# Loading two token tiles as one 2 KB-packet transfer on the second DMA queue, and two weight row blocks as one

## The chip, the cores and the metric

The kernel runs on one NeuronCore of one Trainium2 chip. The metric is the device time of one execution in microseconds, as the median of several runs. Besides, one execution was taken by the hardware profiler; its instructions and transfers are what the profile shows.

## The reference

With x of 2048 tokens by 512 (bf16), the output mixes two branches by a gate for each token:

```python
g = sigmoid((x * gate_w).sum(-1, keepdims=True))
a = A_ref(x, A_wqkv, A_w_phi, A_wo)     # linear attention, 32 heads of 16, softmax feature maps
b = relu(x @ B_w1) @ B_w2               # B_w1: 512 x 1376, B_w2: 1376 x 512
return g * a + (1 - g) * b
```

In A_ref, q, k and v come from x @ wqkv; q and k are multiplied by w_phi for each head and mapped to softmax(p) and softmax(-p), 32 features for each head; then kv is the sum over tokens of phi_k times v, z the sum of phi_k, and the head's output is (phi_q kv) / (phi_q z + 1e-6), which wo projects. Every token's row of the output depends on its own row of x and on sums over all tokens (kv and z), so the order in which tokens stand in a tile does not matter as long as the output rows are put back where they belong.

## The kernel before

The 2048 tokens are 16 tiles of 128, in four chunks of 512. The kernel wants x transposed (XT: features on the partitions). Chunks 1 to 3 come by transposing DMAs (x1, x2, x3). Chunk 0 is wanted first and goes another way: its four tiles m = 0 to 3 are loaded as they are (x00 to x03, into XN, which lies in a buffer FT that is used for other things later), TensorE multiplies each 128 x 128 block by the identity (xt{m}0 and xt{m}1, line 350), ScalarE and VectorE copy the result from PSUM to XT (xe{m}0, line 362, and xe{m}1, line 365).

The first matrix product is h = x W1. W1 is loaded in pieces: columns 0 to 511 by row blocks of 128 (w1a0 to w1a3, 128 KB each), then columns 512 to 1023 in one load of 512 KB (w1b), then the rest (w1c). For the first 256 tokens and the first four column blocks the sum over the row blocks j is spread out, so that TensorE can begin with what has landed: hh00 and hh01 (row block 0, tiles 0 and 1), then hh1, hh2 and hh3 (row blocks 1, 2 and 3 for both tiles; line 405). Then hr0, hr1 and h0_0 to h0_3 (line 411) do the other 256 tokens for these columns, tile 2 (and with it xe20 and xe21) being the first that hr0 needs. h0_4 and on (line 391) take whole chunks; f1_0 to f1_3 (line 374) are folds of the k projection with w_phi, and pr_k0 and on (line 512) the projections. Before any data are there, TensorE does six matmuls on constants (warm0, line 258).

Work is a list of named tasks. Each engine runs its tasks in an order written out by hand (ORDER, lines 17 to 62), and a task waits on semaphores for those tasks of other engines, and those DMAs, that it depends on. DMAs are issued by SP and by ScalarE ("act"), each with its own queue; the transposing loads, too, stand in SP's list. The orders that matter here begin so:

```python
    "sp":  "x00 w1a0 w1a2 x02 x03 w1b wphi wkT w1c wv x1 x2 wqT x3 gw w2a w2b wo ...
    "act": "x01 w1a1 w1a3 xe00 xe10 xe20 xe30 rl0_0 ...
    "pe":  "warm0 xt00 xt01 xt10 xt11 hh00 hh01 hh1 hh2 xt20 xt21 xt30 xt31 hh3 hr0 hr1 h0_0 ...
```

The list g.follow(...) at line 429 repeats part of the order as a constraint. Later parts (features on VectorE, ScalarE and GpSimd, kv, num and den, the output tiles oe{m} and their stores st{m} at line 692) are not touched, but for two stores' addresses. A buffer of stored outputs (OSB) has five slots.

Of the kernel before, what the change touches and what calls it, by code (L numbers as in the profile page):

```python
# [15 lines left out]

ORDER = {
# [4 lines left out]
    ),  # L22
# [5 lines left out]
    ),  # L28
    "act": (
# [20 lines left out]
    ),  # L50
# [98 lines left out]
def bass_gated_mix__linear_kernel_hedgehog__dense_activation_relu__prompt_kernel(  # L149
# [11 lines left out]
    x2 = A_x.rearrange("b s d -> (b s) d")  # L161
    o2 = out.rearrange("b s d -> (b s) d")
    S, D = x2.shape
    H, DH = A_w_phi.shape[0], A_w_phi.shape[1]
    DFF = B_w1.shape[1]
    P = 128
    NT = S // P
    ND = D // P
# [11 lines left out]
    NPB, NTS, NF, NSL = 3, 3, 4, 3  # L180
    NPH, NOM, NOT, NOS = 7, 3, 4, 5
# [6 lines left out]
    with ExitStack() as es:  # L188
        E = es.enter_context

        def sb(name, shape, dt):
            return E(nc.sbuf_tensor(name, shape, dt))
# [6 lines left out]
        W1 = sb("W1", [P, ND, W1C], BF16)  # L199
# [7 lines left out]
        FT = sb("FT", [P, NF, 2 * F], BF16)  # L207
# [3 lines left out]
        OSB = sb("OSB", [P, NOS, D], BF16)  # L211
# [20 lines left out]
        PS = E(nc.psum_tensor("PS", [P, 8, 512], FP32))  # L232
        EPS = 8 * 512

        def ap(t, row, off, dims):
            return bass.AP(tensor=t, offset=off, ap=[[row, P]] + [list(d) for d in dims])

        def psap(off, dims):
            return ap(PS, EPS, off, dims)

        g = _Graph()
        add = g.add
# [5 lines left out]
            boost=700.0)  # L248
        add("ones", "pool", lambda q: q.memset(
            ap(VS, NT * NG * GZ, GV, [[GZ, NT * NG], [1, 1]]), 1.0), dur=0.7, boost=-1e4)  # L250
        add("hpad", "pool", lambda q: q.memset(HR[:, :, :, KREM:P], 0.0), dur=0.6, boost=-1e4)
        XN = FT[:, NF - 2, :].rearrange("p (m d) -> p m d", d=D)
# [13 lines left out]
        def after_last(name, eng):  # L266
            if eng in queue:
                g.follow(queue[eng], name)
            queue[eng] = name

        def load(name, eng, out_, in_, deps=(), dur=0.1, lat=6.0, **how):
            add(name, eng, lambda q: q.dma_start(out=out_, in_=in_, **how), deps, dur=dur, lat=lat, dma=True,
                boost=1e4)
            after_last(name, eng)
# [6 lines left out]
        def chunk(c):  # L281
            return slice(c * 512, (c + 1) * 512)

        w1r = B_w1.rearrange("(j p) n -> p j n", p=P)
        x0r = x2[chunk(0), :].rearrange("(m p) d -> p m d", p=P)
        wvr = A_wqkv[:, 2 * D:3 * D].rearrange("(j p) n -> p j n", p=P)
        def load_x(m, eng, lat):
            load(f"x0{m}", eng, XN[:, m, :], x0r[:, m, :], dur=0.45, lat=lat)

        def load_w(j, eng, lat):  # L290
            load(f"w1a{j}", eng, W1[:, j, 0:512], w1r[:, j, 0:512], dur=0.45, lat=lat)
# [2 lines left out]
        load_x(1, "act", 3.1)  # L294
        load_w(0, "sp", 3.2)
        load_w(1, "act", 3.4)
        load_w(2, "sp", 3.8)
        load_w(3, "act", 3.95)
        load_x(2, "sp", 4.0)
        load_x(3, "sp", 3.9)  # L300
        load("w1b", "sp", W1[:, :, 512:1024], w1r[:, :, 512:1024], dur=0.5, lat=5.0)
        load("wphi", "sp", WPS[:, :, :], A_w_phi.rearrange("(g hl) r c -> (hl r) g c", g=ND), dur=0.5, lat=4.9)
        load_t("wkT", WT[:, ND:2 * ND, :], A_wqkv[:, D:2 * D], (), 4.1, 2.7)
# [21 lines left out]
            ("shift",), dur=0.2)  # L325
        add("mk", "dve", lambda q: q.tensor_tensor(
            MK[:, :], ROWM[:, :], ap(COLH, P, 0, [[DH, GH]]), ALU.is_equal), ("row4", "iota_c"), dur=0.2)
        for j in range(ND):
            add(f"wbd{j}", "dve", lambda q, j=j: q.tensor_tensor(
# [18 lines left out]
        def pe_xt(q, m, n):  # L348
            for j in range(2 * n, 2 * n + 2):
                last = q.matmul(PS[:, XB[m][j // 2], (j % 2) * P:(j % 2 + 1) * P], XN[:, m, j * P:(j + 1) * P],  # L350
                                IDN[:, :], start=True, stop=True)
            return last

        for m in range(4):
            for n in range(2):
                add(f"xt{m}{n}", "pe", lambda q, m=m, n=n: pe_xt(q, m, n),
                    (f"x0{m}", "ident", f"xe{m - 2}{n}" if m > 1 else None), dur=0.2, boost=9000.0 - 10 * m)
            for n, eng in enumerate(("act", "dve")):
                xo = XT[:, 2 * n:2 * n + 2, m * P:(m + 1) * P]
                xi = PS[:, XB[m][n], 0:2 * P].rearrange("p (j t) -> p j t", j=2)  # L360
                if eng == "act":
                    add(f"xe{m}{n}", eng, lambda q, o=xo, i=xi: q.activation(o, i, ACT.Copy), (f"xt{m}{n}",), dur=0.35,
                        boost=9000.0 - 10 * m)
                else:
                    add(f"xe{m}{n}", eng, lambda q, o=xo, i=xi: q.tensor_copy(o, i), (f"xt{m}{n}",), dur=0.37,
                        boost=9000.0 - 10 * m)
        x0 = [f"xe{m}{n}" for m in range(4) for n in range(2)]
# [35 lines left out]
        def pe_h_first(q, j, c0, c1):  # L403
            for k in range(4):
                last = q.matmul(PS[:, GB4[k], c0:c1], W1[:, j, k * P:(k + 1) * P], XT[:, j, c0:c1],  # L405
                                start=(j == 0 and c0 == 0), stop=(j == ND - 1), skip_group_check=True)
            return last
# [10 lines left out]
        add("hh01", "pe", lambda q: pe_h_first(q, 0, P, 2 * P), ("xe10", "hh00"), dur=0.22, boost=8500.0)  # L418
        prev = "hh01"
        for j in range(1, ND):  # L420
            add(f"hh{j}", "pe", lambda q, j=j: pe_h_first(q, j, 0, 2 * P), (f"xe0{j // 2}", f"xe1{j // 2}", f"w1a{j}", prev), dur=0.44,
                boost=8500.0)
            prev = f"hh{j}"

        for k in range(2):
            add(f"hr{k}", "pe", lambda q, k=k: pe_h_rest(q, k, 2 * P, 3 * P, True), ("xe20", "xe21", prev), dur=0.22,
                boost=8200.0)
            prev = f"hr{k}"
        for line in (("warm0", "xt00", "xt01", "xt10", "xt11", "hh00", "hh01", "hh1", "hh2", "xt20", "xt21", "xt30", "xt31",
                      "hh3", "hr0", "hr1"), ("xe00", "xe10", "xe20", "xe30"),  # L430
                     ("ident", "shift", "xe01", "xe11", "xe21", "xe31", "blk", "row4", "mk")):
            for a, b in zip(line, line[1:]):
                g.follow(a, b)
# [8 lines left out]
        for n, (kind, a, k) in enumerate(units):  # L442
            b = GB4[n] if n < 4 else FB[2] if n == 4 else HB[(n - 4) % len(HB)]
            if kind == "h":
                halved = n < 4
                deps = [*xof[a], *w1of[k], prev, *freed[b]]
                if k == KT - 1:
                    deps.append("gw")
                    add(f"h{a}_{k}", "pe", lambda q, a=a, b=b: pe_h_tail(q, a, b), deps, dur=0.69)
                    prev = f"h{a}_{k}"  # L450
# [4 lines left out]
                        out=HT[:, KT - 1, chunk(a)].rearrange("p (n t) -> p n t", t=P),  # L455
                        in_=HR[:, a % 2, :, :].rearrange("p n k -> p (n k)")),
# [9 lines left out]
                    deps, dur=(0.22 if k < 2 else 0.44) if halved else 0.87,  # L466
                    boost=8000.0 if n < 3 else 0.0)
                prev = f"h{a}_{k}"
# [3 lines left out]
            else:  # L472
                deps = ["wqT", *wbd, prev, *freed[b]]
                add(f"f{a}_{k}", "pe", lambda q, a=a, k=k, b=b: pe_fold(q, a, k, b), deps, dur=0.24, boost=1000.0)
                prev = f"f{a}_{k}"
# [4 lines left out]
        for j in range(ND):  # L480
# [3 lines left out]
                boost=1800.0)  # L484
# [11 lines left out]
        for m in range(NT):  # L496
            def add(*a, boost=20.0 * (len(widths) * 2 - m // 2 - VLAG), **how):
                return g.add(*a, boost=boost, **how)
# [18 lines left out]
        for jn, (kind, tiles) in enumerate(jobs):  # L517
            w = len(tiles)
            n = kind_n[kind]
# [59 lines left out]
            else:  # L579
# [4 lines left out]
                    dur=0.11 + 0.207 * w)  # L584
# [6 lines left out]
                for n2, m in enumerate(tiles):  # L591
                    add(f"tq{m}", "sp", lambda q, m=m, fs=fs, n2=n2: q.dma_start_transpose(
                        out=PHQ[:, m % NPH, :, :], in_=FT[:, fs, n2 * F:(n2 + 1) * F]),
                        (f"nm_{J}", *((f"nd{m - NPH}_0", f"nd{m - NPH}_1") if m >= NPH else ())), dur=1.3, lat=2.3, dma=True)
                    if n2 == 0 and m == 0:

                        for b in range(2):
# [9 lines left out]
                                out=o, in0=i, scalar=5e-7, in1=k, op0=ALU.add, op1=ALU.mult),  # L607
                                (f"kv{NT - 1}", "mk"), dur=0.2)
                for m in tiles:
                    for hf in range(2):  # L610
# [3 lines left out]
                        def pe_nd(q, m=m, hf=hf, nb=nb):  # L614
# [11 lines left out]
                            out=OTM[:, m % NOM, hf * 256:(hf + 1) * 256].rearrange("p (h d) -> p h d", d=DH),  # L626
# [4 lines left out]
                        out=OT[:, m % NOT, :, :], in_=OTM[:, m % NOM, :]),  # L631
# [17 lines left out]
                    if m == NT - 1:  # L649
# [15 lines left out]
                        for h2 in range(2):  # L665
# [13 lines left out]
                            else:  # L679
                                add(f"oe{m}_1", "dve", lambda q, m=m, b=b, cs=cs: q.tensor_scalar(  # L680
                                    OSB[:, m % NOS, cs], PS[:, b, 0:cs.stop - cs.start], OMG[:, m:m + 1], None, ALU.mult), need,
                                    dur=0.4)
                            add(f"st{m}_{h2}", ("act", "sp")[h2], lambda q, m=m, cs=cs: q.dma_start(
                                out=o2[m * P:(m + 1) * P, cs], in_=OSB[:, m % NOS, cs]), (f"oe{m}_{h2}",), dur=0.5,
                                lat=1.5, dma=True)
# [4 lines left out]
                        OSB[:, m % NOS, :], PS[:, ab, :], ACT.Copy, scale=OMG[:, m:m + 1]),  # L690
                        (f"a{m}", f"go{m // 4}", f"st{m - NOS}" if m >= NOS else None), dur=0.69)
                    add(f"st{m}", "act", lambda q, m=m: q.dma_start(
                        out=o2[m * P:(m + 1) * P, :], in_=OSB[:, m % NOS, :]), (f"oe{m}",), dur=0.5, lat=1.5, dma=True)

        for then in ("mx_k0", "mn_k0"):
            g.follow("mk", then)
# [41 lines left out]
```

## Time and profile before

| what | value |
|---|---|
| median of 3 runs | 150.18 us (150.1 to 150.44) |
| profiled execution, its own time | 150.59 us |
| its span from first to last instruction | 149.3 us |
| TensorE busy | 146.3 us, 98% of the span |
| VectorE, ScalarE, GpSimd busy | 110.9, 91.8, 109.6 us |
| granted TensorE clock | 1.00 |
| DMA | 16.11 MB, mean 108 GB/s |

In the lines of the profile a time comes first (start in us from the span's begin, then the length), then the engine, the line of the kernel, the operation, the tiles (out<-in, W standing for W1, W2 and the like) and the count; in brackets stands the idle time of the engine before it and what ended it. "SPq" and "ACTq" are the queues' issues of DMAs, PE is TensorE's matmul and PEld its weight load. The DMA view gives the kilobytes and the time from issue to landing. A line of windows has, for each engine, the busy time and the number of instructions, then the granted clock, the busy share of the 16 DMA engines and GB/s.

### The profile page before, as it was taken

To read this page: it belongs to the slowest core of one execution; us is meant where nothing else is said; L and a number is where in the kernel's file an instruction comes from. 1 tells how busy PE (TensorE), PEld (TensorE's weight loads), DVE (VectorE), ACT (ScalarE), POOL (GpSimd) and SP (SyncE) were. 2 spreads that over 40 slices of the span, in tenths; PEclk is the share of its full clock that TensorE was granted. 3 is DMA by queue.
4 is the path that set the end of the run, shared out by engine and by line. 5 is a ranking of instruction groups with operands and counts; after the bars stand their busy time and mean duration, and the time that the engine had idled before them with its cause. 6 is when DMAs were issued, how large, how long until landed. Compare 5 with 4: busy or idle time off the path is not lost.

```text
span 149.3 us, 2619 instructions
## 1 busy us (share of the span) xinstructions
PE 146.3 (98%) x1009; PEld 75.9 (51%) x1009; DVE 110.9 (74%) x168; ACT 91.8 (61%) x127; POOL 109.6 (73%) x72
## 2 busy tenths in 40 slices
PE   7999999999999999999999999999999999999994
PEld 2865444444754465445444545455444444445452
DVE  2343666999796948989999997999989988534401
ACT  3374769799979775898983937175573751310151
POOL 4000399999999999999999999999999793150000
PEclk9999999999999999999999999999999999999999
DMA  5999999900030001000000094646778687656552
GB/s 144 303 234 247 171 212 211 341 27 0 7 70 0 0 4 37 0 0 4 0 0 0 2 111 104 141 103 139 121 169 190 159 212 97 156 134 159 63 156 91
DMA packets 46364, 16.11 MB, mean 108 GB/s; under 512 B 39856, under 2 KB 46352, under 8 KB 46352
## 3 DMA queue, kind: packets, MB, share of 16 engines
q1 hardware_dynamic: 43616, 13.50, 43.2%
q10 hardware_dynamic: 2736, 2.45, 5.1%
q8 instruction: 8, 0.13, 0.4%
q14 instruction: 4, 0.03, 0.1%
HBM read 4.41 MB, written 2.10 MB: 44 GB/s over the span
## 4 chain that ended last, share of the span: by engine, by line
PE 98%; DVE 0%; issue 0%
PE PS L638 24%; PE PS L391 21%; PE PS L512 19%; PE PS L492 9%; PE PS L644 9%; PE PS L573 3%; PE PS L616 3%; PE PS L399 2%; PE PS L405 2%; PE PS L258 2%; PE PS L659 2%; PE PS L411 1%; PE PS L374 1%; PE PS L350 1%; PE PS L670 1%; DVE OSB L680 0%
## 5 line engine op out<-in xcount | busy, mean ns | idle before, releaser
L552 POOL TENSOR_TENSOR TS<-PB,MX 128x1024 bf16<-128x1024 bf16 (+1 forms) x18 | 30.9, 1723 | 15.0 <-DVE MX L543 15.0
L638 PE MATMUL PS<-W,HT 128*128 128x512 bf16 (+1 forms) x165 | 38.1, 379 | 0.0
L559 DVE TENSOR_REDUCE ZB<-FT 128x128 f32<-128x2048 bf16 (+1 forms) x18 | 36.6, 2031 | 1.8 <-ACT FT L557 1.8
L557 ACT ACTIVATE FT<-TS 128x2048 bf16<-128x2048 bf16 (+1 forms) x18 | 30.9, 1718 | 8.7 <-POOL TS L552 8.5
L391 PE MATMUL PS<-XT,W 128*128 128x512 bf16 x144 | 34.7, 379 | 0.0
L552 POOL TENSOR_TENSOR TS<-MN,PB 128x1024 bf16<-128x1024 bf16 (+1 forms) x18 | 30.9, 1725 | 0.8 <-DVE MN L545 0.8
L512 PE MATMUL PS<-WP,XT 128*128 128x512 bf16 x128 | 30.6, 379 | 0.0
L566 POOL TENSOR_TENSOR FT<-FT,SC 128x2048 bf16<-128x2048 bf16 (+1 forms) x9 | 29.5, 3287 | 0.0
L469 ACT ACTIVATE HT<-PS 128x512 bf16<-128x512 f32 x40 | 22.6, 597 | 5.6 <-PE PS L391 4.6
L638 PEld LDWEIGHTS PS<-W,HT 128*128 128x128 bf16 (+1 forms) x165 | 15.5, 98 | 17.1
L689 ACT ACTIVATE OSB<-PS,OMG 128x512 bf16<-128x512 f32 x15 | 10.2, 687 | 22.4 <-PE PS L644 22.3
L543 DVE TENSOR_REDUCE MX<-PB 128x64 bf16<-128x1024 bf16 (+1 forms) x18 | 19.5, 1084 | 6.0 <-ACT PB L539 6.0
L545 DVE TENSOR_REDUCE MN<-PB 128x64 bf16<-128x1024 bf16 (+1 forms) x18 | 19.3, 1084 | 3.2 <-ACT PB L539 3.2
L391 PEld LDWEIGHTS PS<-XT,W 128*128 128x128 bf16 x144 | 13.8, 98 | 15.3
L539 ACT ACTIVATE PB<-PS 128x1024 bf16<-128x1024 f32 (+1 forms) x18 | 16.7, 927 | 7.3 <-PE PS L512 4.2
L512 PEld LDWEIGHTS PS<-WP,XT 128*128 128x128 bf16 x128 | 12.0, 98 | 13.6 <-DVE WP L344 0.4
L492 PE MATMUL PS<-WV,XT 128*128 128x512 bf16 x64 | 16.4, 379 | 0.0
L589 POOL TENSOR_TENSOR FT<-FT,SR 128x1024 bf16<-128x1024 bf16 (+1 forms) x9 | 15.7, 1739 | 0.7
L644 PE MATMUL PS<-WO,OT 128*128 128x512 bf16 x60 | 14.7, 379 | 0.0
L625 DVE SCALAR_TENSOR_TENSOR OTM<-PS,EG,RD 128x256 bf16<-128x256 f32 x32 | 13.8, 463 | 0.4 <-DVE RD L623 0.2
L623 DVE RECIPROCAL RD<-PS 128x16 f32<-128x16 f32 x32 | 6.4, 232 | 9.0 <-PE PS L616 8.8
L501 ACT ACTIVATE VS<-PS 128x512 bf16<-128x512 f32 x16 | 9.6, 602 | 4.3 <-PE PS L492 4.3
(54 smaller groups left out, 106.0 us busy)
## 6 DMA issues: line engine op xcount, KB each, us to landing
out_dram<-OSB ACTq DMA_DIRECT2D x15, 128.0 KB, 2.1
W<-in_B_w_dram SPq DMA_DIRECT2D x1, 1280.0 KB, 6.9
W<-in_B_w_dram SPq DMA_DIRECT2D x1, 512.0 KB, 4.9
WV<-in_A_wqkv_dram SPq DMA_DIRECT2D x1, 512.0 KB, 4.7
WO<-in_A_wo_dram SPq DMA_DIRECT2D x1, 512.0 KB, 7.2
FT<-in_A_x_dram SPq DMA_DIRECT2D x3, 128.0 KB, 3.8
W<-in_B_w_dram SPq DMA_DIRECT2D x1, 352.0 KB, 3.9
W<-in_B_w_dram ACTq DMA_DIRECT2D x2, 128.0 KB, 3.7
```

Source lines behind the costliest of these rows:

```text
L391: last = q.matmul(PS[:, b, :], W1[:, j, k * P:(k + 1) * P], XT[:, j, chunk(c)], start=(j == 0), stop=(j == ND - 1))
L469: add(f"rl{a}_{k}", "act", lambda q, a=a, k=k, b=b: q.activation(HT[:, k, chunk(a)], PS[:, b, :], ACT.Relu), (prev,), dur=0.6, boost=RL)
L492: last = q.matmul(PS[:, 2, :], XT[:, j, m * P:(m + 1) * P], WV[:, j, :], start=(j == 0), stop=(j == ND - 1))
L512: last = q.matmul(PS[:, n, :], XT[:, j, m * P:(m + 1) * P], WP[:, s, j, :], start=(j == 0), stop=(j == ND - 1))
L543: add(f"mx_{J}", "dve", lambda q, sl=sl, w=w, i=pbg: q.tensor_reduce(MX[:, sl, 0:w * H], i, AX.X, ALU.max), (f"ev_{J}", old("t1")), dur=0. ...
L545: add(f"mn_{J}", "dve", lambda q, sl=sl, w=w, i=pbg: q.tensor_reduce(MN[:, sl, 0:w * H], i, AX.X, ALU.min), (f"ev_{J}", old("t2")), dur=0. ...
L552: add(f"{tn}_{J}", "pool", lambda q, o3=o3, a3=a3, b3=b3: q.tensor_tensor(o3, a3, b3, ALU.subtract), (f"{'mx' if sg == 0 else 'mn'}_{J}", ...
L557: add(f"ex_{J}", "act", lambda q, fs=fs, ts=ts, w=w: q.activation(FT[:, fs, 0:w * F], TS[:, ts, 0:w * F], ACT.Exp), (f"t1_{J}", f"t2_{J}", ...
L559: add(f"sm_{J}", "dve", lambda q, fs=fs, sl=sl, w=w: q.tensor_reduce(ZB[:, sl, 0:2 * w * H], FT[:, fs, 0:w * F].rearrange("p (g d) -> p g ...
L566: add(f"nm_{J}", "pool", lambda q, f3=f3, sl=sl, w=w: q.tensor_tensor(f3, f3, SC[:, sl, 0:2 * w * H].unsqueeze(2).to_broadcast([P, 2 * w * ...
L638: last = q.matmul(PS[:, ab, :], HT[0:r, k, m * P:(m + 1) * P], W2[0:r, k, :], start=(k == 0), stop=False)
L644: last = q.matmul(PS[:, ab, :], OT[:, m % NOT, t, :], WO[:, t, :], start=False, stop=(t == ND - 1))
```

## The change

Three things belong together. Row blocks 2 and 3 of W1 (columns 0 to 511) come in one load of 256 KB on SP's queue (still called w1a2; w1a3 is gone). Tiles 2 and 3 of x come in one load of 256 KB (x0b) on ScalarE's queue, in the place of w1a3: partition p takes tokens 256 + 2p and 257 + 2p, which lie side by side in memory, so that a packet has 2 KB; tile 2 then holds the even tokens of these 256 and tile 3 the odd ones, and the stores of tiles 2 and 3 write to every second row. On TensorE the transposes of tiles 2 and 3 stand before hh2 instead of behind it.

```diff
@@ ORDER
     "sp": (
-        "x00 w1a0 w1a2 x02 x03 w1b wphi wkT w1c wv x1 x2 wqT x3 gw w2a w2b wo hx0 hx1 hx2 tq0 tq1 "
+        "x00 w1a0 w1a2 w1b wphi wkT w1c wv x1 x2 wqT x3 gw w2a w2b wo hx0 hx1 hx2 tq0 tq1 "
...
     "act": (
-        "x01 w1a1 w1a3 xe00 xe10 xe20 xe30 rl0_0 rl0_1 rl0_3 rl0_2 rl0_4 fe1_1 fe1_3 rl0_5 ev_k0 rl0_8 rl0_6 "
+        "x01 w1a1 x0b xe00 xe10 xe20 xe30 rl0_0 rl0_1 rl0_3 rl0_2 rl0_4 fe1_1 fe1_3 rl0_5 ev_k0 rl0_8 rl0_6 "
...
     "pe": (
-        "warm0 xt00 xt01 xt10 xt11 hh00 hh01 hh1 hh2 xt20 xt21 xt30 xt31 hh3 hr0 hr1 h0_0 h0_1 h0_2 h0_3 h0_4 "
+        "warm0 xt00 xt01 xt10 xt11 hh00 hh01 hh1 xt20 xt21 xt30 xt31 hh2 hh3 hr0 hr1 h0_0 h0_1 h0_2 h0_3 h0_4 "
@@ the kernel
+        def stored(m):
+            if m in (2, 3):
+                return o2[2 * P:4 * P, :].rearrange("(p n) d -> p n d", n=2)[:, m - 2, :]
+            return o2[m * P:(m + 1) * P, :]
...
         load_w(1, "act", 3.4)
-        load_w(2, "sp", 3.8)
-        load_w(3, "act", 3.95)
-        load_x(2, "sp", 4.0)
-        load_x(3, "sp", 3.9)
+        load("w1a2", "sp", W1[:, 2:ND, 0:512], w1r[:, 2:ND, 0:512], dur=0.45, lat=3.8)
+        load("x0b", "act", FT[:, NF - 2, 2 * D:4 * D], x2[2 * P:4 * P, :].rearrange("(p m) d -> p (m d)", m=2),
+             dur=0.45, lat=3.9)
...
-                    (f"x0{m}", "ident", f"xe{m - 2}{n}" if m > 1 else None), dur=0.2, boost=9000.0 - 10 * m)
+                    (f"x0{m}" if m < 2 else "x0b", "ident", f"xe{m - 2}{n}" if m > 1 else None), dur=0.2, boost=9000.0 - 10 * m)
...
-            add(f"hh{j}", ..., (f"xe0{j // 2}", f"xe1{j // 2}", f"w1a{j}", prev), dur=0.44,
+            add(f"hh{j}", ..., (f"xe0{j // 2}", f"xe1{j // 2}", f"w1a{min(j, 2)}", prev), dur=0.44,
...
-        for line in (("warm0", "xt00", "xt01", "xt10", "xt11", "hh00", "hh01", "hh1", "hh2", "xt20", "xt21", "xt30", "xt31",
+        for line in (("warm0", "xt00", "xt01", "xt10", "xt11", "hh00", "hh01", "hh1", "xt20", "xt21", "xt30", "xt31", "hh2",
                       "hh3", "hr0", "hr1"), ("xe00", "xe10", "xe20", "xe30"),
...
-                        out=o2[m * P:(m + 1) * P, :], in_=OSB[:, m % NOS, :]), (f"oe{m}",), dur=0.5, lat=1.5, dma=True)
+                        out=stored(m), in_=OSB[:, m % NOS, :]), (f"oe{m}",), dur=0.5, lat=1.5, dma=True)
```

More of the change, by code (lines that the diff above doesn't have):

```diff
@@ L420, in bass_gated_mix__linear_kernel_hedgehog__dense_activation_relu__prompt_kernel @@
         for j in range(1, ND):
-            add(f"hh{j}", "pe", lambda q, j=j: pe_h_first(q, j, 0, 2 * P), (f"xe0{j // 2}", f"xe1{j // 2}", f"w1a{j}", prev), dur=0.44,
+            add(f"hh{j}", "pe", lambda q, j=j: pe_h_first(q, j, 0, 2 * P), (f"xe0{j // 2}", f"xe1{j // 2}", f"w1a{min(j, 2)}", prev), dur=0.44,
                 boost=8500.0)
```

## The prediction

> **What bounds the kernel now.** I read the page first, then the timeline of the first ten microseconds engine by engine, then the landings of single loads (the DMA view on a window that holds one issue).
>
> ```profile
> span 149.3 us, 2619 instructions
> PE 146.3 (98%) x1009; PEld 75.9 (51%) x1009; DVE 110.9 (74%) x168; ACT 91.8 (61%) x127; POOL 109.6 (73%) x72
> PE 98%; DVE 0%; issue 0%
> ```
>
> TensorE is the chain: 98% of the span, from 0.77 us to the end of the last matmul at 147.0. Whatever the change does counts only as far as it shifts TensorE's work. A busy PE can still hide small gaps, because the ends of matmuls are modelled; so I compared the starts of neighbouring matmuls with the pitch of their kind.
>
> ```profile
> 3.44 1.03 PE L350 MATMUL PS<-IDN,FT 128*128 128x128 bf16 x8
> 4.31 2.49 PE L405 MATMUL PS<-XT,W 128*128 128x128 bf16 x16
> 6.64 0.61 PE L350 MATMUL PS<-IDN,FT 128*128 128x128 bf16 x8
> 7.09 0.60 PE L405 MATMUL PS<-XT,W 128*128 128x256 bf16 x4
> 7.61 1.68 PEld L411 LDWEIGHTS PS<-XT,W 128*128 128x128 bf16 x24 [0.20 <-ACT XT L362]
> 7.64 1.93 PE L411 MATMUL PS<-XT,W 128*128 128x128 bf16 x24
> ```
>
> These are, in order, xt00 to xt11, then hh00 to hh2, then xt20 to xt31, hh3, and hr0 with what follows. Two things are to be seen. The same eight transposes take 1.03 us at 3.4 and 0.61 at 6.6: less the last one's own 0.31 and 0.22, over seven steps, the pitch is about 0.10 (0.107 when steady) early and 0.056 late. The four matmuls of hh2 start at 6.00, 6.21, 6.42 and 6.54, so TensorE doubles its speed near 6.42 (the granted clock reads 1.00 throughout and does not tell of it). And hr0 starts at 7.64, where the last matmul of hh3, started at 7.42 with a pitch of 0.11, had room for it at 7.53: a gap of 0.11, spent on the eviction of tile 2 (xe20, xe21). From there to the end only two other gaps are over 0.1: 0.12 before pr_k0 (12.89 to 13.01, "DVE WP L344") and 0.15 at 106.7 (a transposed OT tile).
>
> ```profile
> 0.74 0.40 SPq L272 DMA_DIRECT2D FT<-in_A_x_dram  x1
> 1.20 0.89 SPq L272 DMA_DIRECT2D W<-in_B_w_dram  x2
> 2.13 0.91 SPq L272 DMA_DIRECT2D FT<-in_A_x_dram  x2
> 3.08 0.43 SPq L272 DMA_DIRECT2D W<-in_B_w_dram  x1
> 1.18 0.95 ACTq L272 DMA_DIRECT2D W<-in_B_w_dram  x2
> 2.15 1.28 ACT L362 ACT_TABLE_LOAD   x1 [2.15 <-issue]
> ```
>
> ```profile
> W<-in_B_w_dram SPq DMA_DIRECT2D x1, 128.0 KB, 3.9
> W<-in_B_w_dram ACTq DMA_DIRECT2D x1, 128.0 KB, 4.2
> FT<-in_A_x_dram SPq DMA_DIRECT2D x1, 128.0 KB, 3.8
> W<-in_B_w_dram SPq DMA_DIRECT2D x1, 512.0 KB, 4.9
> ```
>
> The last fence has w1a2, w1a3, x03 and w1b alone. Issue plus latency gives the landings: w1a2 5.6, w1a3 5.9, x02 6.1 (also 3.9 after its issue at 2.13), x03 6.4, w1b 8.0. TensorE asks for them at 6.0, 7.1, 6.65, 6.87 and 9.4. Every load is in time, but x02 and x03 by only half a microsecond.
>
> ```profile
> 3.00:4.00 1.00, 1.00 (x8) 0.56 (x7) 0.00 (x0) 0.56 (x2) 0.00 (x0) 1.00 1.18 346
> 4.00:5.00 1.00, 1.00 (x12) 0.82 (x10) 0.85 (x2) 0.64 (x2) 0.00 (x0) 1.00 0.93 277
> 5.00:6.00 1.00, 1.00 (x9) 0.75 (x7) 0.00 (x0) 0.00 (x0) 0.00 (x0) 1.00 1.05 325
> 6.00:7.00 1.00, 1.00 (x12) 0.85 (x11) 0.00 (x0) 0.04 (x1) 0.00 (x0) 1.00 1.13 347
> ```
>
> The last two columns say that the 16 DMA engines are full (0.93 to 1.18) at 277 to 347 GB/s: landings here are set by bytes, hardly by the time of issue. The sixteen parts of x03 land from 5.34 to 6.41, those of w1a2 from 4.42 to 5.60: some engines run 1.1 us behind the quickest, and a load is complete only with the last.
>
> **The change, part by part.** *Issue.* SP loses two issues (0.91 us from 2.13); one load of 256 KB costs one issue (w1b's 512 KB took 0.43, no more than 128 KB). So w1b, wphi, wkT and all behind them on SP go out some 0.95 us earlier. Nobody on TensorE waits for them now (w1b is 1.4 us early, wkT landed at 9.92 for folds at 11.13), so this is worth 0. ScalarE still issues three loads; if the third costs anything between 0.40 and 0.52 (the span of these rows), the table load still ends before xe00 at 3.87, which has 0.43 to spare: 0.
>
> *Order on TensorE.* hh2 moves behind the transposes. hr0 now has hh2 and hh3 (2 x 0.44) between xt31 and itself, while xe20 and xe21 were done 0.9 us after xt20 started: the 0.11 gap goes. Gain 0.11. The evictions xe30 and xe31 are covered in the same way. No other instruction is added; the stores of tiles 2 and 3 go to every second row, still 1 KB each and 128 KB in all, mid-kernel, where a store lands in 2.1 us and nobody waits: 0 (bounds: the slot of OSB is asked for five tiles later, some 13 us).
>
> *The new need.* xt20 now follows hh1 directly: its inputs are wanted at 6.00 instead of 6.65, and both tiles come in one load, so xt20 also waits for what was x03. A landing reaches TensorE in 0.04 us (x00: issue 0.74 plus 2.7, weight load at 3.44). When does the pair land? It leaves at 1.67 in place of w1a3, beside w1a2's 256 KB on SP. Early bound: w1a3 landed at 5.9 from this place with half the bytes; were the pair served like that, there is no stall. Late bound of plain order: pair and w1a2 complete the same 1 MB that x03 completed at 6.41. 2 KB packets are in no row; in the trace's packet records 1 KB took 46 ns and 704 B 34 (medians), which makes some 84 ns by the straight line against 2 x 46, 0.06 us less over the eight of each DMA engine. I take 6.35, the late bound less that, since bytes decide. Stall: 6.39 - 6.00 = 0.39.
>
> *Its price.* Before 6.42 TensorE is slow, so a stall there pushes work into the quick stretch and costs only 0.056/0.107 = 0.52 of its length: 0.39 x 0.52 = 0.20. From 6.42 on it costs all of it. hh2 then needs w1a2's 256 KB: xt20 to xt31 take 0.45 to 0.6 us after the pair, and the row blocks end with the same megabyte, so this is covered; uncovered, it would cost what the row blocks come later than 6.8.
>
> [...]
>
> *Sum.* -0.11 + 0.20 = +0.09 us. Against the profiled execution (150.59: span 149.3 and 1.3 around it) that is 150.68; the median of the runs is 0.41 lower, 150.18, and takes the same difference: **150.27**. What a measurement of this kernel can tell from no change is about 0.2%, 0.3 us; this is inside it. Break-even is a stall of 0.22, a landing at 6.18.
>
> **Rivals.** *In time (0.15).* The pair lands by 5.96: only the gap's end is left, 150.07. For: w1a3's 5.9 and the quickest parts of x03 at 5.34. Against: the 1.1 us by which the last engines lag. With the forecast's case (landing 5.97 to 6.57, sum -0.11 to +0.29, chance 0.32) it makes "within 0.2%".
>
> *The pair comes late (0.25).* Slower by more than 0.3 when it lands after 6.57. Mechanism: w1b's 512 KB now stand in SP's queue a microsecond earlier and compete with ScalarE's pair, where before nothing of w1b came ahead of x03. At 6.9: 0.42 x 0.52 + 0.52 - 0.11 = +0.63, 150.81; at 7.2 +0.93, 151.1. Worst bound, the pair after all of w1b (8.0): 151.9. For: 277 GB/s while both queues work, 347 with SP's alone. Against: w1b is behind w1a2 in its own queue.
>
> *The clock restarts (0.18).* The doubling at 6.42 comes 3.0 us after the last idle stretch (3.29 to 3.44, the wait for x00). Smaller pauses (0.04) at 4.3 and 4.7 did not hold it up. If an idle stretch of 0.15 or more starts the count anew, a pair later than 6.1 does so: quick only from 6.39 + 3.0. The 3.0 us of slow work do 1.56 us of quick work by 9.39, a point that the run of before, without its gap, reached at 7.76: 1.63 lost, less 0.11: 151.70. Against: the first 2.5 us of warm-up were not enough and what counts (unbroken time or a share of a window) is not shown.
>
> [...]
>
> *More gaps go (0.10).* If the earlier loads also took away the 0.12 before pr_k0 and the 0.15 at 106.7, the sum is -0.38: 149.80. Against: the first hangs on evictions of folds, the second on a late transpose; neither is among the loads moved.
>
> **How the numbers follow.** Faster by over 0.2%: 0.10, the last rival. Within: 0.15 + 0.32 = 0.47. Slower: 0.25 + 0.18 = 0.43. The likeliest case is the forecast, whose own range is 150.07 to 150.47. The range goes from 149.75 (all gaps gone) to 151.1 (pair at 7.2) and leaves out the restarted clock.
>
> **What the profile after would show.** L411's weight load without a wait on ACT and starting right behind hh3; L350's second eight starting at 6.0 to 6.4 with a wait for "DMA FT<-in_A_x_dram"; the pair's issue on ACT at 1.67 with a latency near 4.7; w1b issued near 2.1. L350's second eight at 0.056 from 6.42 would refute the restart; at 0.107, still with hh2 behind them slow, it would show it. A start at 6.6 or later makes the forecast wrong, and so does a gap at hr0 that stays.

## The result, and the profile after

The changed kernel takes 151.6 us (median of 9 runs, 150.48 to 153.15) against 150.44 for the kernel before beside it (9 runs, 150.03 to 150.85): ratio 1.0077, interval 1.0049 to 1.0105. It is slower, by more than the forecast's case allowed and beyond the top of the range (151.1). The ratios leave out single executions that took over 1.5% longer than the fastest of their set, here the one at 153.15.

The page of the profiled execution (151.37 us):

```profile
span 150.0 us, 2599 instructions
PE 144.7 (96%) x992; PEld 75.3 (50%) x1009; DVE 110.9 (74%) x168; ACT 91.8 (61%) x127; POOL 109.5 (73%) x72
PE 93%; DMA 4%; issue 1%; ACTq 1%; DVE 0%
```

TensorE is no longer the whole chain: 4% of the span now hang on a DMA (the chain runs back through the pair's whole load, from its issue on, so this is more than the wait). The timeline of TensorE, and its windows, say where (lines from 258 on have moved by four or five: L354 is the transposes, L409 hh00 to hh3, L415 hr0):

```profile
3.41 1.03 PE L354 MATMUL PS<-IDN,FT 128*128 128x128 bf16 x8
4.28 1.34 PE L409 MATMUL PS<-XT,W 128*128 128x128 bf16 x12
7.03 0.62 PE L354 MATMUL PS<-IDN,FT 128*128 128x128 bf16 x8 [1.41 <-DMA FT<-in_A_x_dram]
7.49 1.04 PE L409 MATMUL PS<-XT,W 128*128 128x256 bf16 x8
8.36 0.83 PE L415 MATMUL PS<-XT,W 128*128 128x128 bf16 x12
```

```profile
4.00:5.00 1.00, 1.00 (x13) 0.82 (x11) 0.85 (x2) 0.61 (x2) 0.00 (x0) 1.00 0.94 284
5.00:6.00 1.00, 0.62 (x7) 0.32 (x5) 0.00 (x0) 0.00 (x0) 0.00 (x0) 1.00 0.97 333
6.00:7.00 1.00, 0.00 (x0) 0.00 (x0) 0.00 (x0) 0.00 (x0) 0.00 (x0) 1.00 1.09 327
```

hh1's last matmul starts at 5.35, its successor could have started at 5.46, and xt20 starts at 7.03: a stall of 1.57 us, ended by the pair, with the DMA engines at 0.97 and 1.09 in the two windows of the stall. The wait ahead of hr0 is gone (hh3's last matmul at 8.25, hr0 at 8.36). The issues and the landings (the DMA view at 1.66 and at 2.2 us):

```profile
1.67 0.45 ACTq L277 DMA_DIRECT2D FT<-in_A_x_dram  x1
1.21 1.40 SPq L277 DMA_DIRECT2D W<-in_B_w_dram  x3
3.19 5.41 SPq L282 DMA_TRANSPOSE WT<-in_A_wqkv_dram  x1
```

```profile
W<-in_B_w_dram SPq DMA_DIRECT2D x1, 256.0 KB, 5.5
FT<-in_A_x_dram ACTq DMA_DIRECT2D x1, 256.0 KB, 5.3
W<-in_B_w_dram SPq DMA_DIRECT2D x1, 512.0 KB, 6.4
```

The pair landed at 1.67 + 5.3 = 7.0, the row blocks at 7.2, though in the run of before all of these bytes were there at 6.41. Their sixteen parts are spread wider than those of w1a2 to x03 before: the pair's from 5.32 to 6.99, the row blocks' from 4.65 to 7.20. Nor were fewer bytes moved: by 6.41 the packet records of the two load queues come to 1315 KB here and to 1316 KB before. Of the pair's 128 packets, 126 were done by then; the last two decided when it was complete.

The profiled times differ by 151.37 - 150.59 = 0.78. The stall gives +1.57, the closed gap -0.11; and TensorE doubled its speed near 4.9 us here, not at 6.42, which gives back 1.5 x 0.48 = 0.72 (a pitch of 0.107 in place of 0.056 loses 0.48 of the time). Sum +0.74. So the profile is accounted for; what had to be found was why both loads came late, and whether they always do.

### The profile page after: what moved, and what is told of

It is laid out like the page before. It is cut to its first block, busy times and chain, and to the rows that moved or that the text cites. A ratio compares the mean times of both kernels' runs of the same rounds, so it can differ in the third digit from the quotient of the medians.

```text
span 150.0 us, 2599 instructions
## 1 busy us (share of the span) xinstructions
PE 144.7 (96%) x992; PEld 75.3 (50%) x1009; DVE 110.9 (74%) x168; ACT 91.8 (61%) x127; POOL 109.5 (73%) x72
## 4 chain that ended last, share of the span: by engine, by line
PE 93%; DMA 4%; issue 1%; ACTq 1%; DVE 0%
PE PS L642 24%; PE PS L395 21%; PE PS L516 18%; PE PS L496 9%; PE PS L648 9%; DMA FT<-in_A_x_dram 4%; PE PS L577 3%; PE PS L620 3%; PE PS L403 2%; PE PS L663 2%; PE PS L378 1%; PE PS L415 1%; PE PS L674 1%; PE PS L409 1%; ACTq L277 1%
## 5 line engine op out<-in xcount | busy, mean ns | idle before, releaser
L642 PE MATMUL PS<-W,HT 128*128 128x512 bf16 (+1 forms) x160 | 37.5, 379 | 0.3
L516 PE MATMUL PS<-WP,XT 128*128 128x512 bf16 x124 | 29.9, 379 | 0.2
L496 PE MATMUL PS<-WV,XT 128*128 128x512 bf16 x61 | 15.8, 379 | 0.2
```

The costliest lines, as they stand in the source:

```text
L496: last = q.matmul(PS[:, 2, :], XT[:, j, m * P:(m + 1) * P], WV[:, j, :], start=(j == 0), stop=(j == ND - 1))
L516: last = q.matmul(PS[:, n, :], XT[:, j, m * P:(m + 1) * P], WP[:, s, j, :], start=(j == 0), stop=(j == ND - 1))
L642: last = q.matmul(PS[:, ab, :], HT[0:r, k, m * P:(m + 1) * P], W2[0:r, k, :], start=(k == 0), stop=False)
```

## The experiments

The groups that follow ran on different chips, so each names what ran side by side. *Competition* is my theory: w1b, issued a microsecond earlier, holds up the last parts of the loads issued before it.

**Parts of the change on one chip.** The order alone:

```diff
-warm0 xt00 xt01 xt10 xt11 hh00 hh01 hh1 hh2 xt20 xt21 xt30 xt31 hh3 hr0 ...     (loads as before)
+warm0 xt00 xt01 xt10 xt11 hh00 hh01 hh1 xt20 xt21 xt30 xt31 hh2 hh3 hr0 ...
```

> The loads of before (four row blocks of W1 and four tiles of x by themselves), only TensorE's order of the change: xt20 to xt31 ahead of hh2. Theory 'competition' (the pair is late because w1b's 512 KB, a microsecond earlier on SP's queue, take turns with it): x02 and x03 land at 6.1 and 6.4 as before, the second eight transposes start between 6.0 and 6.4, TensorE stands still for 0.1 to 0.9 us depending on when its speed doubles, ratio to before 0.999 to 1.003. Rival 'order' (asking for tile 2 before hh2 is by itself what costs, whatever the loads): ratio 1.005 or more. Rival 'packets' (the pair's own 2 KB packets or its one completion are slow): as competition.

Ratio 1.0006 (0.9988 to 1.0024): the order alone costs nothing that shows and brings nothing. In its profile xt20 follows hh1 at once, and the eight transposes take 0.80 us because xt30 waits 0.18 for x03 (6.37). A late w1a0 (5.00) also cost about a microsecond ahead of hh00 there (TensorE idle for 0.90), though w1b went out at 3.12, near the 3.08 of before: in this execution a load came late without w1b's earlier issue.

```profile
6.01 0.80 PE L350 MATMUL PS<-IDN,FT 128*128 128x128 bf16 x8
```

The changed kernel with w1b held back:

```diff
-        load("w1b", "sp", W1[:, :, 512:1024], w1r[:, :, 512:1024], dur=0.5, lat=5.0)
+        load("w1b", "sp", W1[:, :, 512:1024], w1r[:, :, 512:1024], ("w1a0",), dur=0.5, lat=5.0)
```

> The changed kernel, but SP issues w1b only when w1a0 has landed (at 4.1 us instead of 2.1), so that no packet of w1b can run beside the pair. Competition: the pair lands by 6.4 on ScalarE's queue, the stall ahead of xt20 shrinks to 0.9 us or less, ratio to before at most 1.003, unless wkT, which goes out later too (about 5.2 us), makes the folds wait by up to 0.4 us. Packets: the pair still lands at 6.6 to 7.2, ratio about 1.007 or more.

Ratio 1.0008 (0.9987 to 1.0028); the pair landed at 6.13 and xt20 waited 0.31. Note that w1a0 holds back more than w1b: wphi and wkT stand behind it on SP and go out later too.

The changed kernel with 1 KB packets:

```diff
-        load("x0b", "act", FT[:, NF - 2, 2 * D:4 * D], x2[2 * P:4 * P, :].rearrange("(p m) d -> p (m d)", m=2),
+        load("x0b", "act", XN[:, 2:4, :], x0r[:, 2:4, :],
...     (the stores of tiles 2 and 3 as before)
```

> The changed kernel with the pair as 256 packets of 1 KB (tile 2 and tile 3 as before in memory and in the stores), still one load on ScalarE's queue. Packets: the pair lands by 6.4, ratio 1.000 to 1.003. Competition: it lands at 6.6 to 7.2 as in the changed kernel, ratio 1.005 to 1.010.

Ratio 1.0042 (1.0001 to 1.0083), with times in two clumps (150.1 to 150.6 and 151.35 and up). The range of neither theory was met, and smaller packets show no gain over the changed kernel beside them (1.0021, next run). The profiled execution was one of the first clump, its pair at 6.06.

The changed kernel again:

> The changed kernel once more, to see what in its profile is steady. Competition and packets: the pair lands at 6.6 to 7.2 again and xt20 starts with it. If instead the late landing was a chance of one execution, it lands anywhere from 6.0 on. The doubling of TensorE's speed (6.42 before, 4.9 in the changed kernel's profile) is expected at another time again if it is not tied to the kernel's own work; if it is tied, near 4.9.

Ratio 1.0021 (0.9993 to 1.0049): on this chip the loss is much smaller than in the first result, and too small to be told from the run with w1b held back (1.0008). Its profile had the pair at 5.74 and no stall, with the doubling near 6.7, so one profile decides nothing on a landing. The theory needed a chip on which the loss is plain.

**Another chip, with more runs.**

> The changed kernel as it is, with more runs, beside the next three. Competition (w1b's early packets on SP's queue hold up the last parts of the pair and of the row blocks): ratio to before between 1.002 and 1.008, with single runs up to 152 that before does not have. Chance alone (the DMA engines lag now and then whatever is queued): the same tail in the next two kernels as well.

Ratio 1.0168 (1.0128 to 1.0208), a loss twice the most that was expected. The pair landed at 7.74 and the row blocks at 7.92. First the line of the timeline at which xt20 starts, then the windows behind it:

```profile
7.78 0.62 PE L354 MATMUL PS<-IDN,FT 128*128 128x128 bf16 x8 [1.98 <-DMA FT<-in_A_x_dram]
```

```profile
8.00:9.00 1.00, 1.00 (x14) 0.85 (x12) 0.78 (x3) 0.66 (x2) 0.00 (x0) 0.81 0.97 86
9.00:10.00 1.00, 1.00 (x8) 0.82 (x7) 0.66 (x4) 0.00 (x0) 0.00 (x0) 0.50 0.94 200
10.00:11.00 1.00, 1.00 (x12) 1.00 (x11) 0.57 (x4) 0.00 (x0) 0.00 (x0) 0.50 1.19 225
11.00:12.00 1.00, 1.00 (x9) 0.82 (x8) 0.00 (x0) 0.90 (x2) 0.00 (x0) 0.50 0.72 117
12.00:13.00 1.00, 0.95 (x8) 0.70 (x8) 0.00 (x0) 0.46 (x2) 0.00 (x0) 0.98 1.08 351
```

Here a second price appears. The column of the granted clock, 1.00 in every window shown so far, falls to 0.50 from 8.6 to 12.0: TensorE stood still for 2.14 us and soon afterwards lost half its speed for (0.19 + 3 x 0.50 + 0.02) / 0.50 = 3.4 us. The time adds up: stall 2.14, half speed 3.4 x 0.48 = 1.64, gap -0.11, earlier doubling (5.2) -0.58: +3.09. By pr_k0 TensorE is 16.13 - 13.01 = 3.12 behind the run of before; the rest of the kernel is 0.16 shorter, which is not taken apart, and the times differ by 153.55 - 150.59 = 2.96. Five of the six executions of this run had a mean clock of 0.988 or 0.989, and took 152.95 to 153.62; the one at 1.00 took 151.84. So much of the 1.0168 is this second price: 151.84 alone is 1.009 of the median of before beside it (150.49).

Now w1b, and with it wphi and wkT, waits for x00, which puts its issue at 3.47, near the 3.08 of before; everything else is the change:

```diff
-        load("w1b", "sp", W1[:, :, 512:1024], w1r[:, :, 512:1024], dur=0.5, lat=5.0)
+        load("w1b", "sp", W1[:, :, 512:1024], w1r[:, :, 512:1024], ("x00",), dur=0.5, lat=5.0)
```

> The changed kernel, but SP issues w1b only when x00 has landed (about 3.2 us; before issued it at 3.1, the changed kernel at 2.1). All else as changed: one pair of 2 KB packets, one load of row blocks, the new order. Competition: the tail is gone, ratio 0.998 to 1.002, the middle one of the pair's sixteen parts lands by 5.3 us (5.16 with w1b behind w1a0; 5.44 to 5.69 in the three with w1b at 2.1). Chance or the loads themselves: ratio and tail as in the changed kernel.

Ratio 1.0020 (1.0002 to 1.0037), far from 1.0168 beside it: nearly all of the loss goes with the issue time of w1b and of what stands behind it. Those two, wphi and wkT, are a rival that none of the runs parts from w1b wholly, but their packets (32 and 256 bytes) first run at 6.49 and 6.68 in the run at 1.0168: by then the pair, complete at 6.30 in the run beside it, was late already. The pair landed at 6.30, the stall is 0.35 (timeline):

```profile
6.34 0.62 PE L354 MATMUL PS<-IDN,FT 128*128 128x128 bf16 x8 [0.18 <-DMA FT<-in_A_x_dram]
```

The part of the expectation on the middle one of the pair's sixteen parts missed: it came at 5.78, against 6.08 in the run beside it. The last part moved by far more, from 7.74 to 6.30. What made the last parts late in the run at 1.0168 is in part single slow packets: between 3.4 and 6.5 us, 18 packets took over 0.3 us each there, 11.2 in all, against 10 and 5.3 here, where the median of a 1 KB packet is 0.046; and by 6.41 it had moved 1109 KB, the run here 1271. Whether w1b's packets cause this or chance does, one execution each cannot show.

The loads of the change with the order of before (the order's diff above, turned round):

> The loads of the change, TensorE's order of before: hh2 directly behind hh1, the transposes of tiles 2 and 3 behind it. Competition: the row blocks land as late as the pair, so hh2 waits for them instead of xt20; ratio 1.002 to 1.008 with the same tail. If only asking for the pair early cost, the ratio would be 0.999 to 1.002.

Ratio 1.0135 (1.0087 to 1.0183), again more than expected. So it is not the order. Now hh2 waits, for the row blocks (7.36), nearly as long as xt20 did in the first profile: hh1's last matmul starts at 5.82 and its successor could at 6.03, which makes 1.47 us:

```profile
7.50 0.60 PE L409 MATMUL PS<-XT,W 128*128 128x256 bf16 x4 [1.40 <-DMA W<-in_B_w_dram]
```

And the supposed cause added to the kernel before:

```diff
-    "sp":  "x00 w1a0 w1a2 x02 x03 w1b wphi ...          "act": "x01 w1a1 w1a3 xe00 ...
+    "sp":  "x00 w1a0 w1a2 x02 x03 wphi ...              "act": "x01 w1a1 w1a3 w1b xe00 ...
-        load("w1b", "sp", ...
+        load("w1b", "act", ...
```

> The kernel before with one thing added: w1b goes out on ScalarE's queue behind w1a3, at about 2.1 us, while x02 and x03 stay on SP at 2.1 and 2.6. ScalarE's table load moves back by one issue (0.45 us), to an end near 3.9, where xe00 starts now. Competition: w1b's 512 KB run beside x02 and x03, whose last parts land after 6.6 and up to 7.5 instead of 6.1 and 6.4; xt20 or xt30 wait, ratio 1.002 to 1.010 with runs above 151. Chance: ratio 0.999 to 1.002.

Ratio 1.0102 (1.0074 to 1.0131), with four single 128 KB loads and the old order. x02 landed at 2.13 + 5.2 = 7.4 and x03 at 2.60 + 5.5 = 8.1, w1a2 at 6.67, each more than a microsecond later than in the profile of before, and w1a2 landed before any packet of wphi or wkT ran (6.68 and 6.88). The DMA view at 2.13 and at 2.6 us, then the timeline, in which hh2 waits for w1a2:

```profile
FT<-in_A_x_dram SPq DMA_DIRECT2D x1, 128.0 KB, 5.2
FT<-in_A_x_dram SPq DMA_DIRECT2D x1, 128.0 KB, 5.5
```

```profile
6.80 0.60 PE L405 MATMUL PS<-XT,W 128*128 128x256 bf16 x4 [1.24 <-DMA W<-in_B_w_dram]
```

**Candidates and the form of the competition, on a third chip.** Order of the change with the loads of before, w1b behind w1a0; before with w1b behind w1a0; w1b on ScalarE's queue behind the pair ("x01 w1a1 x0b w1b"); the changed kernel with w1b behind w1a0:

> A candidate: the loads of before, TensorE's order of the change, and w1b issued only when w1a0 has landed (about 4 us). Competition: x02 and x03 land by 6.1 with nothing of w1b beside them, the gap ahead of hr0 is gone, ratio 0.996 to 1.000. Chance alone: 1.000 to 1.002 as with the order alone (1.0006).

> The kernel before with w1b issued only when w1a0 has landed (about 4 us instead of 3.1). Competition: the loads of before already have half a microsecond to spare, so hardly anything moves: ratio 0.997 to 1.001. If the later w1b and what stands behind it on SP were a cost of their own, above 1.002.

> The changed kernel with w1b on ScalarE's queue directly behind the pair (issue at 2.1 us as in the changed kernel), the row blocks alone on SP's queue up to then. Two forms of the competition part here. Turns: a DMA engine takes turns between its two queues, so that w1b slows the pair when it stands in the other queue; then behind the pair it no longer does, the pair lands by 6.4 and only the row blocks come late. Shared: the quick DMA engines, done with both, go on to w1b and take what the slow ones would need; then the pair and the row blocks both land after 6.6 as in the changed kernel, with nothing of w1b ahead of them in either queue; ratio 1.004 to 1.017.

> The changed kernel with w1b behind the landing of w1a0, once more with more runs. Competition: ratio 0.998 to 1.003, no run above 152 and no run with a granted clock under 1; pair at 6.0 to 6.4. Chance: the tail of the changed kernel shows here too.

Ratios 1.0027 (1.0002 to 1.0053), 1.0017 (0.9991 to 1.0042), 1.0008 (0.9981 to 1.0035) and 1.0043 (1.0017 to 1.0070). No candidate beats the kernel before, and none of the four expectations was met in full: three ratios lie above what competition allowed, and with w1b behind the pair (1.0008) pair and row blocks landed at 5.90 and 6.08, where one form had the row blocks late and the other both. The changed kernel as it is did not run here, so this chip does not say whether there was a loss to cure. Holding w1b back as far as w1a0 can have a price of its own, seen in the profile of the last of them, though that execution (150.30) is not one of the longer ones (up to 151.79), whose cause stays open: wkT, behind it on SP, lands at 10.95 and the folds wait (0.36 us between matmuls), since the quick start of that execution (doubling near 4.9) had brought TensorE there early.

```profile
10.99 0.90 PEld L378 LDWEIGHTS PS<-WBD,WT 128*128 128x128 bf16 x16 [0.69 <-DMA WT<-in_A_wqkv_dram]
```

**All on a fourth chip:**

> The changed kernel, on one chip with the next three. Both forms of competition: the pair and the row blocks land after 6.4, later than in x3; ratio 1.002 to 1.017, with the more, the more the chip's slow DMA engines lag.

> The changed kernel with w1b on ScalarE's queue directly behind the pair. Turns: the pair lands as early as in x3, and the ratio is near that of x3, as long as the row blocks come by 7. Shared: pair and row blocks as late as in x1 and the ratio of x1, give or take 0.002.

> The changed kernel with w1b issued after x00 has landed. Both forms: ratio 0.999 to 1.003 and lower than x1's, pair by 6.4, no execution with the granted clock under 1.

> The kernel before, with a profile from the same chip. Ratio 0.998 to 1.002. The last parts of w1a2, w1a3, x02 and x03 land by 5.9, 6.1, 6.3 and 6.6; if the chip's slow engines lag as much here as in x1 (w1a2 after 6.5), the lag belongs to the chip and not to w1b.

Ratios 1.0072 (1.0038 to 1.0105), 1.0038 (1.0016 to 1.0061), 1.0016 (0.9995 to 1.0037) and 1.0001 (0.9975 to 1.0026). The interval of the changed kernel again lies above that of the same kernel with w1b at 3.4, if barely (1.0038 against 1.0037). The tails say it more plainly: over 153 us are five of 12 executions in x1, three of 12 in x2 and none of 12 in x3, and none of 35 of the kernel before.

The expectation of x4 is the test of the rival "the lag belongs to the chip", and it was met: on this chip the loads of before landed at 5.75, 5.92, 6.20 and 6.53, while w1a2 in x1 came at 6.96. It is one execution each, but it agrees with the times.

With w1b behind the pair the ratio lies between the two and overlaps both, so the forms "turns" and "shared" are not told apart by the times. Two things speak for "shared". In the profiled execution of x2 (153.35 us) the pair landed at 7.65 and the row blocks at 7.86, with w1b behind the pair in its own queue and nothing of it on SP. And w1a2 stands ahead of w1b in the same queue in the changed kernel, and still landed at 7.92 and 7.36 with w1b at 2.1 against 6.49 with w1b at 3.4 on one chip, at 6.96 against 6.84 on another; on the first chip, though, at 6.05 and 5.88 against 6.30. Against it stands the third chip, where the pair behind which w1b stood came at 5.90. So the form is argued, not shown. The profile of x3 has the pair at 6.64, hardly sooner than x1's 6.72: again the times, not one landing, carry the verdict.

The execution of x2 also shows the second price again. hh1's last matmul starts at 5.23 and xt20 could start at 5.34; TensorE stands still for 2.36 us, and the clock falls to 0.50 while it waits, for 0.28/0.50 + 2 + 0.43/0.50 = 3.4 us from about 7.45 on:

```profile
7.70 1.03 PE L354 MATMUL PS<-IDN,FT 128*128 128x128 bf16 x8 [2.19 <-DMA FT<-in_A_x_dram]
```

```profile
7.00:8.00 1.00, 0.30 (x4) 0.31 (x5) 0.00 (x0) 0.00 (x0) 0.00 (x0) 0.72 2.61 163
8.00:9.00 1.00, 1.00 (x10) 0.88 (x9) 0.66 (x2) 0.77 (x2) 0.00 (x0) 0.50 0.21 33
9.00:10.00 1.00, 1.00 (x6) 0.71 (x5) 0.58 (x4) 0.00 (x0) 0.00 (x0) 0.50 1.18 194
10.00:11.00 1.00, 1.00 (x12) 0.92 (x10) 0.87 (x5) 0.00 (x0) 0.00 (x0) 0.57 1.33 275
```

Over all chips a mean clock under 0.99 stands beside 10 of 37 executions of the changed kernel, none of 24 with w1b behind x00, and one of 128 of the kernel before.

## Why the prediction was wrong, by its own steps

*The issue: wrong, and the decisive step.* I booked the earlier issue of w1b, wphi and wkT at 0 because nobody on TensorE waited for these loads, and took landings as "set by bytes, hardly by the time of issue". What cost was the landing of others: with w1b out at 2.13 instead of 3.08 the engines moved 1315 KB by 6.41, against 1316 before, but pair and row blocks were not complete among them (7.0 and 7.2). On two chips the issue time of w1b, and of wphi and wkT behind it, separates 1.0168 from 1.0020 and 1.0072 from 1.0016; w1b put early into the kernel before gives 1.0102. Whether and how w1b's packets hold up the others stays open. I even had this as the rival "the pair comes late", but discounted it with "w1b is behind w1a2 in its own queue". A queue's order may not protect a load's last parts, as w1a2's landings on two of three chips suggest (7.92 and 7.36 with w1b at 2.1 against 6.49 with it at 3.4; 6.96 against 6.84). My reason for the rival was misread, too: of the rows shown, that from 3.00 to 4.00 has 346 GB/s with both queues at work, so the 277 is not the price of two queues. And what stands behind on SP did not all go out earlier: wkT's issue took 5.41 us instead of 3.72, and w1c left at 8.65 instead of 7.88 in these two profiles.

*The new need: right in kind, mis-sized.* xt20 did wait for the pair. The landing was put at 6.35 from the bytes; with w1b early on SP it was 5.74 to 7.74, with w1b later 5.76 to 6.64 (6.35 lies within that). "Bytes decide" failed: the last of the sixteen parts decided (6.99 in the first profile, where the first came at 5.32), and how far it lagged differed from execution to execution. No run puts the pair on SP, so what ScalarE's queue was worth to it is not shown.

*The price of the stall: right as arithmetic, wrong in its premise.* I fixed the doubling at 6.42. In the executions profiled it came anywhere from 3.7 (x1) to 6.7 (the changed kernel again), both of the changed kernel, and early (4.9) in the changed kernel's first profile; then hh1 is done at 5.46, the stall is longer and costs all of its length.

*The order: right.* The gap ahead of hr0 closed; 0.11 us is below what the runs can tell (order alone 1.0006).

*The rival "the clock restarts": right that speed can be lost with a stall, wrong in its trigger of 0.15 us.* In the first profile the second eight transposes run at a pitch of 0.056, the prediction's own sign against a restart. With stalls of up to 1.57 us nothing was set back; with 2.14 us and 2.36 us the clock fell to 0.50, and the price of the first, 1.64 us, is close to the 1.63 worked out. In both the fall came 3.4 us after the doubling (5.2 and 8.62; about 4.05 and 7.45), in one behind the stall and in the other within it. TensorE stood still for 2.1 of these 3.4 us in both, and for 1.57 us where nothing fell. Whether unbroken time or a share of a longer stretch counts, two executions do not show. The loss came with landings that were very late (7.74 and 7.65); it is no case of its own.

## What to carry to other kernels

With the DMA engines busy for 0.87 to 0.98 of the time from 4 to 7 us (the run at 1.0168), issuing a large load earlier was not free here, though nobody waited for it and it stood behind the urgent ones: with w1b at 2.1 in place of about 3.4 us the ratio was 1.0168 against 1.0020 and 1.0072 against 1.0016. Ask which urgent load's last part is still under way. Holding the large one back as far as x00 did not bring the time below the kernel before. Judge a landing by the last of its sixteen parts and over several executions and chips (the pair's, with w1b early on SP, came from 5.74 to 7.74). The reserve of half a microsecond that x02 and x03 had is not what mattered: the order alone spent it and cost nothing (1.0006), and the loads alone lost as much without the order (1.0135). TensorE's speed doubled at 3.7 to 6.7 us in executions of one and the same kernel, so do the sum for an early and a late doubling.

## What the runs showed of the hardware that was not expected

- The sixteen parts of one 256 KB load landed 3.3 us apart (the row blocks in the run at 1.0168: 4.67 to 7.92), with the DMA engines busy for 0.87 to 0.98 of the time from 4 to 7 us.
- The same program lost 0.2%, 0.7%, 0.8% and 1.7% in four sets of runs on at least three chips, while the median of the kernel before stayed at 150.4 to 150.7 in all of them.
- The granted clock fell to 0.50 for 3.4 us shortly after a stall of 2.14 us and during one of 2.36 us, and not with one of 1.57.
- TensorE's speed doubled anywhere from 3.7 to 6.7 us after the start, which by the two pitches (0.107 and 0.056) moves an execution by up to 3.0 x 0.48 = 1.4 us, an estimate.
- The issue of one transposing load (wkT) held SP for 3.72 us in one profile and 5.41 in another with other loads ahead of it.
